# Routing token ids instead of token rows to the experts of a fused attention and mixture-of-experts kernel

## The chip, the cores and the metric

The kernel runs on one core of a Trainium2 chip. A core has a matrix engine (PE, with its weight loads shown apart as PEld), a vector engine (DVE), a scalar engine (ACT), a general engine (POOL), and a sync engine (SP), which here only issues DMAs. Each engine runs its own instructions in the order in which the program gives them. DMAs that SP issues are made into transfers by hardware; indirect DMAs, whose row numbers stand in a tile, are issued by POOL, which itself works out the transfers. All of them are carried by the same 16 DMA engines.

The metric is the device time of one execution in microseconds (us), lower is better. All times below are in us.

## The reference

The first half is a gated linear attention over a state of 48 x 48 for each of 4 batches and 8 heads, 768 steps long. Its output, taken as 3072 tokens of 384 numbers, goes into a mixture of 8 experts with one expert for each token. A token whose skip score is not positive passes unchanged.

```
for t in range(S):                                     # S = 768; B, H, D = 4, 8, 48
    state = alpha[:, :, t, :, None] * state + einsum('bhd,bhe->bhde', k[:, :, t], v[:, :, t])
    y[:, :, t] = einsum('bhd,bhde->bhe', q[:, :, t], state)
x = y.transpose(0, 2, 1, 3).reshape(B * S, H * D)      # 3072 tokens of 384

do_compute = x @ w_skip > 0
xc = x[do_compute]
e_idx = argmax(xc @ w_gate);  gate_w = softmax(xc @ w_gate)[e_idx]
for e in range(8):                                     # w1[e]: 384 x 1024, w2[e]: 1024 x 384
    h = maximum(xc[e_idx == e] @ w1[e], 0)
    y[e_idx == e] = gate_w * (h @ w2[e])
out = x;  out[do_compute] = xc + y
```

## The kernel before

**Attention.** The 3072 tokens are 24 blocks of 128 (`NT`), and one pass of the loop in `static_path` (lines 780 to 848) handles one block. `load(i + 4)` fetches the inputs of a later block on SP: for the first five blocks one transfer of 112 rows of 1541 numbers (L217), afterwards two (L220), and the 128 x 384 values (L223). There are five input buffers. `decay(i + 3)` scans the decay factors twice on DVE (L233, L241) and multiplies keys and queries by them, on POOL from block 2 on (L244, L245). `scores`, `causal`, `inter`, `intra`, `outer` and `carry` are the attention itself, on PE, DVE and ACT. `rows(i - 1)` turns a block's result into 128 rows of 384 numbers, copies them to the tile `x` (ACT, L343) and writes them to `out` (SP, L345). So every token's row is in `out` before any expert runs, as the result of a token that no expert handles, and in the tile `x` as well.

**Routing.** `route_expert` or `route_one` finds the expert and the gate of each token; `route_rank` and `route_slot` number the tokens of an expert one after the other. Expert e owns a stretch of the scratch tensor `xs` in DRAM; its first 256 places (`CAP`) are its slots. `scatter(i)` (POOL, L474) sends the 128 rows of `x`, 386 numbers each (384 of the token, its row number, its gate), to their slots by an indirect DMA. A slot that gets no token must hold a row number that is out of range, so that nothing is written for it at the end: `clear_pieces` fills all slots beforehand with `empty`, whose row number is `OFF`. It makes `empty` on POOL (L146, L147) and issues eight transfers on SP, two in each of the first four passes of the loop.

**Expert 0.** Most tokens of expert 0 are fetched early: in the last pass `early_rows` reads its 256 slots into `xr0` (SP, L435) as soon as the scatters of the first 21 blocks have landed. `early_turn` transposes them on PE (L449). The tokens of the last three blocks (`LATE` on) are added to the transposed tile by a product with a 0/1 matrix (`late_rows`, `hot`), and needn't come through DRAM. For this the tile `slots0` holds the slot number of each column.

**Experts.** `gather(e)` reads the 256 slots of an expert into `xr`, two transfers of 128 rows on SP (L530). Expert 1 and 0 come first, and then `gather(e + 2)` at the head of each expert's pass. An expert's pass is, in the written order of each engine:

- `gather(e + 2)`;
- four times `up(e, g)`: 18 matrix products of about 0.12 us on PE into one of three `ps_h` buffers, then `hh` on ACT (L581) and `hl` on DVE (L582), which frees the buffer; behind each, two pieces of `split_pieces(e + 1)`: ACT makes the high part of a raw weight piece (L508) and DVE or POOL the low part (L512). Of the 12 pieces POOL does numbers 1, 3, 6, 8 and 11; 0 to 5 belong to `w1`, 6 to 11 to `w2`;
- `turn(e + 1)`: transposes the next expert's rows (PE, L557);
- four raw `w1` pieces of expert e + 2 on SP (L492, 128 x 768 numbers each). They go into the buffer that the raw `w1` of expert e + 1 occupies, and are issued when all its readers on ACT, DVE and POOL are done;
- twice `down(e, j)`: 24 products on PE (L593), then `o` = gate times the result plus the token's row on DVE (L596), and an indirect DMA of 128 rows to `out` by the row numbers (POOL, L598); two more weight pieces behind each, and one step of `guard`;
- four raw `w2` pieces of expert e + 2 on SP.

`guard` looks for decay factors out of the range that the fast path may use. It reads all of `alpha` in eight portions through a single buffer (SP, L541, 128 x 1152 numbers each), and ACT passes over each portion twice (L545); the next portion is issued when both are done. It spans experts 0 to 4.

The order is the written one (`manual_schedule`). Waits follow from what instructions read and write. Scatters to one tensor are declared independent of each other (`disjoint`), and readers of `xs` are made to wait for them by `after`.

## Time and profile before

| | |
|---|---|
| time, three runs | 328.18, 332.03 (median), 335.56 |
| time of the profiled execution | 333.48 |
| its span in the profile | 331.8 |
| PE busy | 292.5 (88%) |
| DVE busy | 226.9 (68%) |
| POOL busy | 184.3 (56%) |
| ACT busy | 152.6 (46%) |
| moved by DMA | 66.15 MB, of these 4.83 MB by POOL's indirect DMAs |
| attention and routing | 0 to about 182 |
| the eight experts | about 182 to 325 |

A row of a timeline gives the start of an instruction from the start of the span, its duration, engine, line and operation, what it writes and reads, its shape, and how many such instructions were merged into the row. In square brackets stands the time for which the engine had been idle and what ended that. "SPq" is SP issuing a DMA: its duration is that of the issue, not of the transfer. A row of the windows gives for each engine the busy time in a stretch with the number of instructions, then the granted share of the PE clock, the mean share in which the 16 DMA engines were busy, and the rate in GB/s. The chain of waits follows the work that ended last back from the end.

### The profile page before, as it was taken

What the parts mean: (1) busy time and instruction counts of PE and PEld (TensorE: products, weight loads), DVE (VectorE), ACT (ScalarE), POOL (GpSimd) and SP (SyncE); (2) the same over time, 40 slices, a digit from 0 to 9 for tenths busy, and PEclk for the clock granted to TensorE, in tenths of its full rate; (3) what the DMA queues carried; (4) which work ended last, traced back from release to release, by engine and by line L of the source; (5) the groups of instructions that cost most, each with busy time, mean ns of one, the idle gap of its engine ahead of it and who ended that gap; (6) DMA issues with size and microseconds to landing.
All of it is one profiled execution on the core that took longest, in us unless ns stands there. A gap on an engine that the chain in (4) does not pass through costs nothing. (4 is left out here: it accounts for less than half of the span.)

```text
span 331.8 us, 7365 instructions
## 1 busy us (share of the span) xinstructions
PE 292.5 (88%) x2778; PEld 270.2 (81%) x2778; DVE 226.9 (68%) x453; ACT 152.6 (46%) x298; POOL 184.3 (56%) x205
## 2 busy tenths in 40 slices
PE   5877879998699986858898999999999999999991
PEld 5766768887588775646677999999999899999991
DVE  8995578899979999999437664738183555455320
ACT  5122422353435414402424657958595976455200
POOL 6093432589888988866524445444655355464311
PEclk9578785999879999995959999999999999999997
DMA  7949999999976867773546574949688586751000
GB/s 230 281 133 250 252 283 250 223 257 224 236 148 152 183 157 176 197 193 97 155 125 201 166 235 157 398 137 379 215 285 314 193 331 229 242 172 63 12 19 29
DMA packets 29420, 66.15 MB, mean 199 GB/s; under 512 B 4466, under 2 KB 15456, under 8 KB 29376
## 3 DMA queue, kind: packets, MB, share of 16 engines
q1 hardware_dynamic: 26816, 60.76, 63.6%
q0 software_dynamic: 2560, 4.83, 4.2%
q8 instruction: 24, 0.39, 0.5%
q14 instruction: 20, 0.16, 0.2%
HBM read 52.87 MB, written 15.77 MB: 207 GB/s over the span
## 5 line engine op out<-in xcount | busy, mean ns | idle before, releaser
L254 PE MATMUL ps_s<-qka 48*128 48x128 f32 x384 | 31.8, 308 | 23.8 <-POOL qka L244 12.0
L244 POOL TENSOR_TENSOR qka<-qka,sfx 112x512 f32<-112x512 f32 x22 | 27.7, 1257 | 42.4 <-DVE sfx L241 30.7
L254 PEld LDWEIGHTS ps_s<-qka 48*128 48x128 f32 x384 | 26.9, 209 | 29.0 <-POOL qka L244 13.5
L582 DVE SCALAR_TENSOR_TENSOR hl<-ps_h,hh 128x512 fp32r<-128x512 f32 x32 | 22.1, 690 | 33.5 <-ACT hh L581 33.3
L593 PE MATMUL ps_o<-w2h,hh 128*128 128x384 f32 x128 | 43.6, 341 | 0.0
L598 POOL DMA_INDIRECT out_dram<-o,xr x16 | 18.6, 1162 | 45.0 <-DVE o L596 45.0
L593 PE MATMUL ps_o<-w2h,hl 128*128 128x384 f32 x128 | 43.0, 336 | 0.0
L593 PE MATMUL ps_o<-w2l,hh 128*128 128x384 f32 x128 | 43.0, 336 | 0.0
L233 DVE TENSOR_TENSOR_SCAN pfx<-qka,seed 112x516 f32<-112x516 f32 x24 | 34.0, 1418 | 11.0 <-DMA qka<-in_qka_dram 11.0
L343 ACT COPY x<-ps_g 128x384 f32<-128x384 f32 x23 | 11.0, 480 | 65.5 <-DVE logit L338 23.7
L512 POOL TENSOR_TENSOR w2l<-raw,w2h 128x512 fp32r<-128x512 f32 x24 | 31.2, 1302 | 13.5 <-ACT w2h L508 13.1
L474 POOL DMA_INDIRECT xs<-x,slot x24 | 29.9, 1244 | 12.2 <-DVE on L386 4.9
L577 PE MATMUL ps_h<-xh,w1h 128*128 128x256 f32 x192 | 34.2, 284 | 1.2 <-DVE hl L582 1.2
L310 ACT COPY xt<-ps_y 48x512 f32<-48x512 f32 x48 | 27.8, 580 | 13.6 <-PE ps_y L305 12.8
L577 PE MATMUL ps_h<-xh,w1l 128*128 128x256 f32 x192 | 33.8, 282 | 0.0
L241 DVE TENSOR_TENSOR_SCAN sfx<-qka,seedb 112x515 f32<-112x515 f32 x24 | 32.3, 1347 | 1.5
L577 PE MATMUL ps_h<-xl,w1h 128*128 128x256 f32 x192 | 33.3, 282 | 0.0
L305 PE MATMUL ps_y<-st,vt 128*48 128x128 f32 x384 | 32.9, 313 | 0.0
L512 POOL TENSOR_TENSOR w1l<-raw,w1h 128x512 fp32r<-128x512 f32 x16 | 22.3, 1395 | 18.7 <-issue 10.4
L581 ACT ACTIVATE hh<-ps_h 128x512 fp32r<-128x512 f32 x32 | 19.1, 597 | 27.6 <-PE ps_h L577 27.6
L261 DVE COPY_PREDICATED st<-mask,ps_s 128x1024 f32<-128x1024 uint8 x24 | 30.9, 1286 | 0.0
L596 DVE SCALAR_TENSOR_TENSOR o<-ps_o,xr 128x384 f32<-128x384 f32 x16 | 9.9, 616 | 30.3 <-PE ps_o L593 30.3
(141 smaller groups left out, 667.5 us busy)
## 6 DMA issues: line engine op xcount, KB each, us to landing
raw<-in_w_dram SPq DMA_DIRECT2D x64, 384.0 KB
qka<-in_qka_dram SPq DMA_DIRECT2D x38, 288.9 KB
vt<-in_v_dram SPq DMA_DIRECT2D x24, 192.0 KB
out_dram<-x SPq DMA_DIRECT2D x24, 192.0 KB
alpha<-in_nat_dram SPq DMA_DIRECT2D x8, 576.0 KB
xr<-xs SPq DMA_DIRECT2D x18, 193.0 KB
xs<-empty SPq DMA_DIRECT2D x8, 386.0 KB
qka<-in_first_dram SPq DMA_DIRECT2D x3, 674.2 KB
```

The lines of the kernel that those rows point to most:

```text
L233: nc.vector.tensor_tensor_scan(pfx[:PD].rearrange("p a t -> p (a t)"), w["qka"][:PD, 0:n], self.seed1[:PD], 0.0, ALU.mult, ALU.max)
L241: nc.vector.tensor_tensor_scan(sfx[:PD, 0:n - 1][:, ::-1], w["qka"][:PD, 2:AW][:, ::-1], seed[:PD, 2:AW][:, ::-1], 0.0, ALU.mult, ALU.add)
L244: (eng or nc.gpsimd).tensor_tensor(w["kh"][:PD], w["kh"][:PD], after, ALU.mult)
L254: nc.tensor.matmul(ps[:, h, p * P:(p + 1) * P], lhsT=kh[r, p, :], rhs=qh[r, p, :], start=True, stop=True)
L261: self.nc.vector.copy_predicated(w["st"], self.mask, w["ps"])
L305: nc.tensor.matmul(ps[h][64 * h:64 * h + D, p, :], lhsT=v[:, o:o + D], rhs=w["st"][:, h, p * P:(p + 1) * P], start=(i < B and p == 0), sto ...
L310: nc.scalar.copy(out=xt[r], in_=ps[h][r])
L474: ins = nc.gpsimd.indirect_dma_start(out=self.xs[:, :], out_offset=bass.IndirectOffsetOnAxis(ap=self.slot[:, i, :], axis=0), in_=x, in_off ...
L512: eng.tensor_tensor(lo[:, s], raw[:, s], hi[:, s].bitcast(F32), ALU.subtract)
L577: nc.tensor.matmul(ps[:, u, :], lhsT=a[:, k, f * P:(f + 1) * P], rhs=b[:, k, :], start=(n == 0), stop=(n == len(order) - 1))
L582: nc.vector.scalar_tensor_tensor(out=hl, in0=ps, scalar=0.0, in1=hh.bitcast(F32), op0=ALU.max, op1=ALU.subtract)
L593: nc.tensor.matmul(ps, lhsT=a[:, f, js], rhs=b[:, f, :], start=(n == 0), stop=(n == 3 * FT - 1))
```

## The change

The slots hold two numbers, a row number and a gate, instead of 386. `scatter` sends only those two columns of `x`. A reader of an expert's slots first fetches them on SP (`meta`, 128 x 2 x 2 numbers, one transfer instead of two) and then the token rows themselves: `fetch_rows` issues two indirect DMAs on POOL that read 128 rows each from `out` by the row numbers in `meta`. Row numbers out of range are skipped, so the receiving tiles are cleared once: `xr0` on POOL at the start, the three tiles `xrb` on DVE before the experts.

The slots of an expert are laid out anew (partition p holds slots 2p and 2p + 1), and `slots0` follows that.

The eight transfers of `clear_pieces` become one, `clear`, of 8 x 256 x 2 numbers. It is issued as a whole before the loop over the blocks, and followed on SP by three transfers that write zeros to the rows of `out` that belong to the last three blocks, since the early fetch names all of `out` as its source before these rows are written. The loop's calls that advanced the clearing are gone.

A fetch reads `out`, and so waits for what was written there before it (`rows`, and later the experts' results), and what is written there after it waits for the fetch.

```diff
@@ first_constants
-        self.xs = dram.tile([E * N, XW], F32, name="xs")
+        self.xs = dram.tile([E * N, 2], F32, name="xs")
@@ first_slots
-        nc.gpsimd.iota(slots0_i, pattern=[[1, CAP]], base=-int(BIG), channel_multiplier=0)
+        nc.gpsimd.iota(slots0_i, pattern=[[1, NB], [NB, P]], base=-int(BIG), channel_multiplier=0)
@@
-    def clear_pieces(self):
-        nc = self.nc
-        empty = self.const.tile([P, XW], F32, name="empty")
+    def slots(self, e0, e1):
+        return self.xs.rearrange("(e n) w -> e n w", e=E)[e0:e1, :CAP, :].rearrange("e (p j) w -> p e (j w)", j=NB)
+
+    def clear(self):
+        nc = self.nc
+        empty = self.const.tile([P, NB, 2], F32, name="empty")
         nc.gpsimd.memset(empty, 0.0)
-        nc.gpsimd.iota(empty[:, DM:DM + 1].bitcast(I32), pattern=[[0, 1]], base=OFF, channel_multiplier=0)
-        for e in range(E):
-            yield nc.sync.dma_start(out=self.xs[e * N:e * N + CAP, :].rearrange("(j p) w -> p j w", p=P),
-                                    in_=empty.unsqueeze(1).to_broadcast([P, NB, XW]))
+        nc.gpsimd.iota(empty[:, :, 0:1].bitcast(I32), pattern=[[0, NB]], base=OFF, channel_multiplier=0)
+        nc.sync.dma_start(out=self.slots(0, E),
+                          in_=empty.rearrange("p j w -> p (j w)").unsqueeze(1).to_broadcast([P, E, 2 * NB]))
+        for i in range(LATE, NT):
+            row = self.row(i)
+            nc.sync.dma_start(out=self.out[row:row + P, :], in_=self.xr0[:, 0, :])
@@ attention_pools
+        self.xr0 = self.late.tile([P, NB, DM], F32, name="xr0")
+        nc.gpsimd.memset(self.xr0, 0.0)
@@ early_rows
-        for j in range(NB):
-            ins = nc.sync.dma_start(out=self.xr0[:, j, :], in_=self.xs[j * P:(j + 1) * P, :])
-            self.after(ins.ins, "xs")
-            self.early.append(ins.ins.name)
+        meta = self.late.tile([P, NB, 2], F32, name="meta0")
+        ins = nc.sync.dma_start(out=meta.rearrange("p j w -> p (j w)"), in_=self.slots(0, 1).rearrange("p e w -> p (e w)"))
+        self.after(ins.ins, "xs")
+        self.early = [ins.ins.name]
+        self.fetch_rows(self.xr0, meta)
+
+    def fetch_rows(self, xr, meta):
+        for j in range(NB):
+            self.nc.gpsimd.indirect_dma_start(
+                out=xr[:, j, :], out_offset=None, in_=self.out[:, :],
+                in_offset=bass.IndirectOffsetOnAxis(ap=meta[:, j, 0:1].bitcast(U32), axis=0),
+                bounds_check=N - 1, oob_is_err=False)
@@ scatter
-            in_=x, in_offset=None, bounds_check=E * N - 1, oob_is_err=False)
+            in_=x[:, DM:DM + 2], in_offset=None, bounds_check=E * N - 1, oob_is_err=False)
@@ expert_pools
+        self.xrb = [self.mp.tile([P, NB, DM], F32, name=f"xr{i}", bufs=1) for i in range(3)]
+        for t in self.xrb:
+            self.nc.vector.memset(t, 0.0)
@@ gather
-        xr = self.mp.tile([P, NB, XW], F32, name="xr", bufs=3)
-        for j in range(NB):
-            s = e * N + j * P
-            ins = self.nc.sync.dma_start(out=xr[:, j, :], in_=self.xs[s:s + P, :])
-            self.after(ins.ins, "xs")
-        self.ew[e] = dict(xr=xr)
+        xr = self.xrb[e % len(self.xrb)]
+        meta = self.mp.tile([P, NB, 2], F32, name="meta", bufs=4)
+        ins = self.nc.sync.dma_start(out=meta.rearrange("p j w -> p (j w)"),
+                                     in_=self.slots(e, e + 1).rearrange("p e w -> p (e w)"))
+        self.after(ins.ins, "xs")
+        self.fetch_rows(xr, meta)
+        self.ew[e] = dict(xr=xr, meta=meta)
@@ down
-        nc.vector.scalar_tensor_tensor(out=o, in0=ps, scalar=xr[:, j, DM + 1:DM + 2], in1=xr[:, j, 0:DM],
+        nc.vector.scalar_tensor_tensor(out=o, in0=ps, scalar=meta[:, j, 1:2], in1=xr[:, j, :],
...
-            out_offset=bass.IndirectOffsetOnAxis(ap=xr[:, j, DM:DM + 1].bitcast(U32), axis=0),
+            out_offset=bass.IndirectOffsetOnAxis(ap=meta[:, j, 0:1].bitcast(U32), axis=0),
@@ static_path
-            clear = self.clear_pieces()
+            self.clear()
             for i in range(NT):
                 if i + 4 < NT:
                     self.load(i + 4)
-                advance(clear, 2)
```

More of the change, by code (lines that the diff above doesn't have):

```diff
@@ L340, in rows @@
         x = self.xp.tile([P, XW], F32, name="x")
-        row = i % B * S + i // B * P
+        row = self.row(i)
         nc.gpsimd.iota(x[:, DM:DM + 1].bitcast(I32), pattern=[[0, 1]], base=row, channel_multiplier=1)
@@ L586, in down @@
         w2h, w2l = (a.rearrange("p (f m) -> p f m", m=DM) for a in self.wt[e]["w2"][:2])
-        xr = w["xr"]
+        xr, meta = w["xr"], w["meta"]
         js = slice(j * P, (j + 1) * P)
@@ L757, in static_path @@
         ends = {g[1] - 1: g for g in groups}
-        pending, split, fetch, clear = [], iter(()), iter(()), iter(())
+        pending, split, fetch = [], iter(()), iter(())
         def advance(it, n):
```

5 lines of the change are left out of this document (3 added, 2 removed).

## The prediction

> **What bounds the kernel now.** I read the profile's first page, then the windows by stage, the timelines of SP, POOL, ACT and DVE around the edits, and the chain of waits.
>
> ```profile
> span 331.8 us, 7365 instructions
> ```
>
> ```profile
> core 0: us, PE busy (x) PEld busy (x) DVE busy (x) ACT busy (x) POOL busy (x), PEclk, DMA share, GB/s
> 0.00:20.00 20.00, 13.23 (x100) 11.80 (x100) 18.47 (x29) 6.79 (x13) 9.36 (x20) 0.74 0.80 222
> 60.00:160.00 100.00, 84.44 (x1134) 71.93 (x1133) 93.48 (x197) 37.89 (x78) 81.68 (x100) 0.93 0.77 186
> 182.00:235.00 53.00, 53.00 (x380) 52.81 (x379) 30.58 (x47) 38.73 (x72) 26.78 (x21) 1.00 0.72 252
> 235.00:261.00 26.00, 24.84 (x184) 24.43 (x182) 11.96 (x19) 18.40 (x33) 11.65 (x9) 1.00 0.63 221
> 261.00:325.00 64.00, 63.89 (x446) 63.41 (x446) 32.42 (x55) 31.41 (x60) 28.08 (x22) 1.00 0.46 164
> ```
>
> Attention is DVE's (93.48 of 100 us). The experts are PE's: from 182 on it idles only 26 - 24.84 = 1.16 us. So whatever makes PE wait there is paid in full, unless it ends before that 1.16. The profiled execution took 333.48, 1.45 over the median 332.03; I sum against 333.48 and subtract 1.45.
>
> **Part 1, the start.** Two edits pull apart. Eight clearing transfers (128 x 2 x 386 x 4 bytes = 395 KB each, 3.16 MB) become one small one and three of zeros (197 KB each). And the new clearing is issued as a whole ahead of the loop, so ahead of the load of block 4.
>
> ```profile
> 8.69 0.33 SPq L217 DMA_DIRECT2D qka<-in_first_dram  x1
> 20.44 2.37 SPq L149 DMA_DIRECT2D xs<-empty  x2
> ```
>
> ```profile
> 19.79 0.41 POOL L146 MEMSET empty<- 128x386 f32 x1
> 20.28 0.13 POOL L147 IOTA empty<- 128x1 int32 x1
> ```
>
> ```profile
> 20.23 1.22 DVE L233 TENSOR_TENSOR_SCAN pfx<-qka,seed 112x516 f32<-112x516 f32 x1
> 29.05 1.23 DVE L233 TENSOR_TENSOR_SCAN pfx<-qka,seed 112x516 f32<-112x516 f32 x1 [3.25 <-DMA qka<-in_qka_dram]
> ```
>
> ```profile
> DVE pfx L233 <- DMA qka<-in_qka_dram: 10.7, 4, 3.2
> ```
>
> The load of block 4 is issued at 8.69, and SP then stands until POOL has made `empty` (20.41). POOL's queue keeps that place; with a smaller fill I put it at 20.1. Now the load of block 4 (112 x 1541 x 4 = 690 KB) stands behind that wait and behind 590 KB of zeros. The first window moved 222 GB/s at a share of 0.80, 278 when busy: 1.28 MB take 4.6. With 2.4 of fixed delay (the shortest landing quoted in part 2) block 4 is there at 20.1 + 4.6 + 2.4 = 27.1, where DVE took it up at 20.23: 6.9 late. Against that, the four waits for loads of blocks 5 to 8, 10.7 together, were beside the clearing. The first (3.25) falls into the lag anyway. If all four go, the start gains 10.7 - 6.9 = 3.8; if only the first goes, it loses 3.6. From block 6 on, a load is issued behind the row output of an earlier block, which the lag delays too, so I don't take the whole: 2 gained. The smaller scatters (24 x 198 KB gone) I cost at nothing: DVE's 93% from 60 to 160 hides them. `xr0`'s fill on POOL lies under the first loads.
>
> **Part 2, expert 0's early rows.** One transfer on SP and two indirect DMAs on POOL replace two on SP.
>
> ```profile
> 173.08 0.80 SPq L435 DMA_DIRECT2D xr<-xs  x2
> ```
>
> ```profile
> L474 POOL DMA_INDIRECT xs<-x,slot x24: 971/1048/2007, 62.3 to 183.1; - x24
> DMA to landing us min/median/max: 2.4/4.6/5.9
> ```
>
> ```profile
> 177.71 0.61 PE L449 MATMUL ps_s<-ident,xr 128*128 128x128 f32 x4
> 179.95 0.69 PE L449 MATMUL ps_s<-ident,xr 128*128 128x128 f32 x4
> ```
>
> No gather is in this trace; the nearest is the scatter of 128 rows. The row numbers land at 173.08 + 2.4 = 175.5, POOL issues at 175.5 and 176.7, and the rows land 2.4 to 4.6 later: 177.9 to 180.1 and 179.1 to 181.3. PE reads them at 177.71 and 179.95. So 0 to 1.35; I take 0.4. Queued behind the fetch are POOL's low parts of blocks 22 and 23 (about 0.5 late, under PE's own wait) and SP's row outputs and last two raw pieces, needed an expert later.
>
> **Part 3, the expert loop.** Here a wait is added that was not there: POOL must have the row numbers before it can issue. Behind the two fetches in POOL's order stand its pieces of the next expert's weights.
>
> ```profile
> 185.80 2.70 SPq L530 DMA_DIRECT2D xr<-xs  x6
> 191.68 2.13 SPq L492 DMA_DIRECT2D raw<-in_w_dram  x4
> 204.28 1.84 SPq L492 DMA_DIRECT2D raw<-in_w_dram  x4
> 206.23 0.99 SPq L530 DMA_DIRECT2D xr<-xs  x2
> 209.67 1.76 SPq L492 DMA_DIRECT2D raw<-in_w_dram  x4
> 214.95 7.53 SPq L541 DMA_DIRECT2D alpha<-in_nat_dram  x2
> 222.58 1.86 SPq L492 DMA_DIRECT2D raw<-in_w_dram  x4
> ```
>
> ```profile
> 196.96 1.19 POOL L598 DMA_INDIRECT out_dram<-o,xr  x1 [3.24 <-DVE o L596]
> 198.18 1.30 POOL L512 TENSOR_TENSOR w2l<-raw,w2h 128x512 fp32r<-128x512 f32 x1
> 205.36 1.38 POOL L512 TENSOR_TENSOR w1l<-raw,w1h 128x512 fp32r<-128x512 f32 x1 [1.71 <-ACT w1h L508]
> 206.89 1.56 POOL L512 TENSOR_TENSOR w1l<-raw,w1h 128x512 fp32r<-128x512 f32 x1 [0.15 <-ACT w1h L508]
> ```
>
> ```profile
> 201.04 1.26 ACT L545 ACTIVATE over<-alpha,lim 128x1152 bf16<-128x1152 f32 x1 [5.33 <-DMA alpha<-in_nat_dram]
> 219.34 1.26 ACT L545 ACTIVATE over<-alpha,lim 128x1152 bf16<-128x1152 f32 x1 [3.39 <-DMA alpha<-in_nat_dram]
> 221.98 0.58 ACT L581 ACTIVATE hh<-ps_h 128x512 fp32r<-128x512 f32 x1
> 228.07 0.62 ACT L508 CAST w2h<-raw 128x512 fp32r<-128x512 f32 x1 [0.93 <-DMA raw<-in_w_dram]
> 228.91 0.62 ACT L508 CAST w2h<-raw 128x512 fp32r<-128x512 f32 x1 [0.22 <-DMA raw<-in_w_dram]
> ```
>
> ```profile
> 207.95 1.64 DVE L512 TENSOR_TENSOR w1l<-raw,w1h 128x512 fp32r<-128x512 f32 x2
> 222.59 0.69 DVE L582 SCALAR_TENSOR_TENSOR hl<-ps_h,hh 128x512 fp32r<-128x512 f32 x1 [3.52 <-ACT hh L581]
> ```
>
> ```profile
> 200.19 8.66 PE ps_h L577 x72
> 281.31 0.66 PE ps_x L557 x6
> 298.94 0.66 PE ps_x L557 x6
> ```
>
> These rows show a ring of waits with little to spare. SP issues raw `w1` at 209.67, just after DVE's last reading of the old one (207.95 + 1.64 = 209.59; POOL's had ended at 208.45). Behind it stands `alpha` (214.95), which lands 4.39 later; ACT reads it twice, and only then turns to `hh` (221.98), for which PE's buffers wait. Then come the next `alpha` and raw `w2` (222.58). From raw `w2` to raw `w2` that is 222.58 - 204.28 = 18.3; PE needs 298.94 - 281.31 = 17.63 for an expert. Now the same ring after the change, counted from the first raw `w2` issue:
>
> - the row numbers are issued at 206.23 - 204.28 = 1.95, behind four raw pieces in the same queue. Those pieces land 0.84 apart (ACT finds them at 228.07 and 228.91), the first 5.5 after its issue, so the fourth at 8.0 and the row numbers with it. Bounds: 4.35 if a small transfer passes the queue, 8.0 if not. I take 8.0, since the pieces themselves come in order;
> - POOL's two fetches, 198.18 - 196.96 = 1.22 each: 10.45;
> - POOL's two `w1` pieces, 1.38 + 1.56: 13.4. They now end last, and release raw `w1` there (before: 5.4);
> - `alpha` is issued 1.85 after, at 15.25. It lands 4.39 + 1.5 later, as the four pieces ahead carry 4 x 0.84 = 3.36 and had 1.85 of start: 21.15;
> - from the first reading to the next raw `w2` 222.58 - 219.34 = 3.24: 24.4.
>
> So the ring takes 24.4, 6.8 more than PE needs. It turns three times (`alpha` ends in expert 4). Its first delay: the row numbers of expert 1 are issued at 185.80 and land at 188.2; six fetches (experts 1, 0, 2) take 7.3, two pieces 2.94, so raw `w1` goes out at 198.5 instead of 191.68, `alpha` lands at 198.5 + 1.85 + 5.9 = 206.3 instead of 201.04, 5.2 late. `hl` of expert 1 ends 3.94 after the first reading (222.59 + 0.69 - 219.34), at 210.2; PE wants that buffer for its fourth group at 200.19 + 3 x 8.66 / 4 = 206.7: 3.5 of stall. Then 6.8 in each of the experts 2, 3 and 4, together 23.9; less the 1.16 of before, 22.7. The first turn of expert 1 may come up to 2.5 late, and DVE's three fills put `hl` of expert 0 up to 2.3 back; both go into the 3.5. Experts 5 to 7 have no `alpha`, and their raw pieces have a whole expert's time: nothing.
>
> By the Trainium skill (TensorE: Matmul & The Clock Gate, Part 1) an idle window of about 3.4 us halves the PE clock until about 3.4 us of work have passed. The 1.16 of idle time kept 1.00 here, which neither confirms nor denies it; stalls of 6.8 would be long enough. The next stall would absorb the loss, except after the last: an estimate of 1.7 more.
>
> **Sum.** 333.48 - 2 + 0.4 + 22.7 = 354.6; less 1.45, 353.
>
> **Rivals.**
>
> *Row numbers pass the queue.* They land at 4.35, raw `w1` goes out at 9.75, `alpha` lands at 17.5, and the ring takes 20.7: stalls of 3.5 + 3 x 3.1 - 1.16 = 11.6, 342 in all. For it: 2 KB against 393 KB. Against: the order in which raw pieces land.
>
> *Fetches are dear.* If each costs POOL 2.0, the longest scatter, the first delay grows by 6 x 0.78 = 4.7 and the ring by 1.6: 8.2 + 3 x 8.4 - 1.16 = 32.2; with 0.6 more in part 2, 363. For it: the 2007 ns; against: the median of 1048. The Trainium skill (SBUF — State Buffer, "SBUF: two separate sides") says that some DVE operations lock POOL out while it writes the transfers of a DMA.
>
> *Not slower: POOL has room.* If its `w1` pieces still end by 209.59, the ring stays at 18.3 and only the start counts: 330, and 321 if all 10.7 are won and block 4 is not late. This decides where the fetches end by 209.59 - 2.94 = 206.65. For it: POOL is busy 26.78 of 53 us. Against: the row numbers aren't issued before 206.23, so the pieces would have to stand ahead of the fetches, and the written order has them behind.
>
> **How the numbers follow.** Forecast 0.58 (346 to 360), row numbers pass 0.18, dear fetches 0.14, POOL has room 0.10. About 2% (325.4 to 338.6) is what a measurement can tell from no change. Faster than that is only the better end of the last rival, 0.04; within it the rest of that rival and the low tail of the first, 0.09; slower 0.87. The range runs from 339, the first rival with a good start, to 366, where the dear fetches meet a start that gains nothing.
>
> **What would show it.** SP issues block 4's load after 20, and DVE waits some 6 us for it; the waits for blocks 5 to 8 shrink. POOL idles before the fetch of experts 3 to 6 until the row numbers land; raw `w1` follows POOL's second piece, not DVE's; ACT waits longer for `alpha`, and PE idles before the fourth group of experts 1 to 4. I am wrong if POOL doesn't wait there, or if PE stays busy from 182 on.

## The result: 13.6% slower, and the profile after

The changed kernel takes 377.72 us (median of 4 runs) where the kernel before takes 332.57 beside it: ratio 1.1356, interval 1.1051 to 1.1662. The direction was forecast, the size was not: 353, with a range up to 366. Two of its four executions, the profiled one (380.15) among them, ran some 1% longer than the other two, and a ratio leaves such executions out. So times are compared by the ratios, and the rows below for where things stand.

The page of the changed kernel: its span, PE's busy tenths and granted clock, and what the transfers moved, in 40 slices.

```profile
span 378.4 us, 7392 instructions
...
PE   6860989987889978499797969759589399997991
...
PEclk9585796999977999956989989969989889999997
...
GB/s 240 138 52 189 191 250 193 164 233 204 211 145 114 174 142 180 128 115 63 93 125 77 205 172 162 264 206 85 233 231 182 149 206 216 168 194 212 29 4 36
```

The windows by stage, with stretches that answer to those of before (experts from 193 on):

```profile
core 0: us, PE busy (x) PEld busy (x) DVE busy (x) ACT busy (x) POOL busy (x), PEclk, DMA share, GB/s
0.00:20.00 20.00, 14.45 (x100) 12.93 (x100) 18.48 (x28) 6.15 (x12) 9.38 (x20) 0.74 0.63 179
60.00:160.00 100.00, 83.45 (x1127) 71.39 (x1126) 91.26 (x181) 37.29 (x74) 75.07 (x93) 0.93 0.78 171
193.00:246.00 53.00, 44.24 (x308) 43.39 (x307) 29.32 (x37) 24.12 (x45) 26.71 (x23) 0.96 0.51 168
246.00:315.00 69.00, 53.17 (x328) 52.75 (x329) 40.79 (x43) 42.91 (x78) 27.49 (x23) 0.88 0.53 179
315.00:371.00 56.00, 53.26 (x373) 51.99 (x371) 33.75 (x44) 21.55 (x40) 27.01 (x22) 1.00 0.41 140
```

PE now idles in the experts, 8.8 us of the first 53 and 15.8 of the next 69, and its clock falls to 0.88. The experts' first product begins at 193.2 (182.3 before) and their last ends at 370.7 (324.9): 10.9 us lost ahead of them, 34.9 in them.

**The start.** SP's timeline, then DVE's for the first scan of block 4:

```profile
20.78 0.41 SPq L152 DMA_DIRECT2D xs<-empty  x1
21.23 1.54 SPq L157 DMA_DIRECT2D out_dram<-xr  x3
22.82 0.44 SPq L230 DMA_DIRECT2D qka<-in_first_dram  x1
```

```profile
33.34 1.23 DVE L246 TENSOR_TENSOR_SCAN pfx<-qka,seed 112x516 f32<-112x516 f32 x1 [12.37 <-DMA qka<-in_first_dram]
```

The load of block 4, issued at 8.69 before, goes out at 22.82, and its data are taken up 10.5 us later. In that time the transfers nearly stand: the page's third slice (18.9 to 28.4 us) shows 52 GB/s.

**The way into the experts.** POOL's timeline has the two fetches of expert 0's early rows and the last scatter, SP's the row numbers of the experts, and the view of the slots' transfers how long these took to land:

```profile
185.12 1.06 POOL L454 DMA_INDIRECT xr<-out_dram,meta  x1 [2.48 <-DMA meta<-xs]
186.49 1.02 POOL L454 DMA_INDIRECT xr<-out_dram,meta  x1 [0.31 <-issue]
...
192.50 0.97 POOL L494 DMA_INDIRECT xs<-x,slot  x1 [0.31 <-issue]
```

```profile
197.88 1.28 SPq L552 DMA_DIRECT2D meta<-xs  x3
```

```profile
DMA to landing us min/median/max: 1.7/5.5/10.6
```

That view takes in all transfers of the slots, three reads of row numbers among them. The scatters alone whose landing is recorded (20 of the 24) took 5.4 us in the median, 3.4 to 10.6; of those of 1544-byte rows (9 of the 24) it was 4.6, 2.4 to 5.9. So a scatter of 8-byte rows landed no sooner. The last one, issued at 192.50, landed 5.1 us later (2.4 before), and SP can ask for the row numbers only at 197.88.

**The ring.** One turn of it in expert 2, in the timelines of SP, POOL, ACT and PE (PE's first three rows are of passes 0 and 1; pass e is the work on expert e):

```profile
223.69 1.83 SPq L512 DMA_DIRECT2D raw<-in_w_dram  x4
225.57 0.43 SPq L552 DMA_DIRECT2D meta<-xs  x1
236.91 1.75 SPq L512 DMA_DIRECT2D raw<-in_w_dram  x4
238.76 10.49 SPq L565 DMA_DIRECT2D alpha<-in_nat_dram  x2
249.35 0.88 SPq L512 DMA_DIRECT2D raw<-in_w_dram  x2
```

```profile
231.94 1.05 POOL L454 DMA_INDIRECT xr<-out_dram,meta  x1 [14.12 <-DMA meta<-xs]
233.30 1.01 POOL L454 DMA_INDIRECT xr<-out_dram,meta  x1 [0.31 <-PE ps_o L617]
234.33 2.55 POOL L532 TENSOR_TENSOR w1l<-raw,w1h 128x512 fp32r<-128x512 f32 x2
```

```profile
246.12 1.25 ACT L569 ACTIVATE over<-alpha,lim 128x1152 bf16<-128x1152 f32 x1 [10.82 <-DMA alpha<-in_nat_dram]
```

```profile
203.81 0.55 PE L581 MATMUL ps_x<-ident,xr 128*128 128x128 f32 x3 [1.77 <-DMA xr<-out_dram,meta]
205.33 0.55 PE L581 MATMUL ps_x<-ident,xr 128*128 128x128 f32 x3 [0.98 <-DMA xr<-out_dram,meta]
224.44 1.01 PE L601 MATMUL ps_h<-xh,w1h 128*128 128x256 f32 x3 [3.70 <-DVE hl L606]
250.10 1.01 PE L601 MATMUL ps_h<-xh,w1h 128*128 128x256 f32 x3 [6.41 <-DVE hl L606]
```

POOL stands 14 us before the fetch; its two `w1` pieces follow and release raw `w1` (236.91); `alpha` comes behind that, and PE waits 6.4 for the evictions that ACT does after it. The waits of the whole execution, totals first:

```profile
POOL xr L454 <- DMA meta<-xs: 67.2, 6, 14.5
ACT over L569 <- DMA alpha<-in_nat_dram: 43.7, 4, 12.0
...
PE ps_h L601 <- DVE hl L606: 21.8, 4, 6.4
```

### The profile page after: what moved, and what is told of

The parts are those of the page before. It is cut to its first block, busy times and chain, and to the rows that moved or that the text cites. A ratio compares the mean times of both kernels' runs of the same rounds, so it can differ in the third digit from the quotient of the medians.

```text
span 378.4 us, 7392 instructions
## 1 busy us (share of the span) xinstructions
PE 304.8 (81%) x2778; PEld 281.3 (74%) x2778; DVE 256.1 (68%) x456; ACT 152.9 (40%) x298; POOL 200.0 (53%) x224
## 4 chain that ended last, share of the span: by engine, by line
PE 30%; DMA 21%; POOL 16%; DVE 15%; issue 9%; ACT 4%; SPq 3%; POOLq 0%; DVEq 0%; ACTq 0%
PE ps_h L601 8%; DMA alpha<-in_nat_dram 8%; PE ps_o L617 7%; POOL w1l L532 4%; DVE sfx L254 4%; PE ps_s L267 3%; PE ps_g L350 3%; DMA qka<-in_qka_dram 3%; DVE pfx L246 3%; DMA qka<-in_first_dram 3%; PE ps_y L296 3%; DMA raw<-in_w_dram 3%; DVE st L274 3%; SPq L512 2%; POOL xr L454 2%
## 5 line engine op out<-in xcount | busy, mean ns | idle before, releaser
L454 POOL DMA_INDIRECT xr<-out_dram,meta x18 | 18.8, 1047 | 77.8 <-DMA meta<-xs 67.2
L267 PE MATMUL ps_s<-qka 48*128 48x128 f32 x384 | 33.6, 323 | 30.2 <-POOL qka L257 22.6
L267 PEld LDWEIGHTS ps_s<-qka 48*128 48x128 f32 x384 | 28.7, 223 | 36.2 <-POOL qka L257 24.6
L601 PE MATMUL ps_h<-xh,w1h 128*128 128x256 f32 x192 | 37.2, 303 | 21.8 <-DVE hl L606 21.8
L606 DVE SCALAR_TENSOR_TENSOR hl<-ps_h,hh 128x512 fp32r<-128x512 f32 x32 | 22.0, 686 | 42.4 <-ACT hh L605 42.4
L601 PEld LDWEIGHTS ps_h<-xh,w1h 128*128 128x128 f32 x192 | 30.6, 206 | 22.9 <-DVE hl L606 22.7
L532 DVE TENSOR_TENSOR w2l<-raw,w2h 128x512 fp32r<-128x512 f32 x24 | 43.5, 1812 | 2.3 <-ACT w2h L528 2.3
L246 DVE TENSOR_TENSOR_SCAN pfx<-qka,seed 112x516 f32<-112x516 f32 x24 | 32.1, 1338 | 15.2 <-DMA qka<-in_first_dram 12.4
L494 POOL DMA_INDIRECT xs<-x,slot x24 | 31.3, 1306 | 13.1 <-DVE slot L436 6.8
L569 ACT ACTIVATE over<-alpha,lim 128x1152 bf16<-128x1152 f32 x16 | 20.2, 1259 | 43.9 <-DMA alpha<-in_nat_dram 43.7
L601 PE MATMUL ps_h<-xh,w1l 128*128 128x256 f32 x192 | 36.0, 297 | 0.0
L601 PE MATMUL ps_h<-xl,w1h 128*128 128x256 f32 x192 | 35.1, 295 | 0.0
```

The source lines that it names most:

```text
L246: nc.vector.tensor_tensor_scan(pfx[:PD].rearrange("p a t -> p (a t)"), w["qka"][:PD, 0:n], self.seed1[:PD], 0.0, ALU.mult, ALU.max)
L267: nc.tensor.matmul(ps[:, h, p * P:(p + 1) * P], lhsT=kh[r, p, :], rhs=qh[r, p, :], start=True, stop=True)
L454: self.nc.gpsimd.indirect_dma_start(out=xr[:, j, :], out_offset=None, in_=self.out[:, :], in_offset=bass.IndirectOffsetOnAxis(ap=meta[:, j ...
L494: ins = nc.gpsimd.indirect_dma_start(out=self.xs[:, :], out_offset=bass.IndirectOffsetOnAxis(ap=self.slot[:, i, :], axis=0), in_=x[:, DM:D ...
L532: eng.tensor_tensor(lo[:, s], raw[:, s], hi[:, s].bitcast(F32), ALU.subtract)
L601: nc.tensor.matmul(ps[:, u, :], lhsT=a[:, k, f * P:(f + 1) * P], rhs=b[:, k, :], start=(n == 0), stop=(n == len(order) - 1))
```

## The experiments

Each is an edit of the changed kernel. "Experts" is the time from the first product of expert 0 to the last product of expert 7, in the profiled execution; block 9 is where DVE begins the first scan of that block; the ratio is to the kernel before, run beside it on the same chip. "All together" is the row numbers in one transfer, fetches not ordered against scatters, and the mended start. TensorE, VectorE and ScalarE in the expectations are PE, DVE and ACT.

| kernel | ratio (interval) | block 9 | experts begin | experts take |
|---|---|---|---|---|
| before | 1 | 56.5 | 182.3 | 142.6 |
| changed | 1.1356 (1.1051–1.1662) | 62.5 | 193.2 | 177.5 |
| fetches later in the pass | 1.0800 (1.0747–1.0852) | 63.1 | 190.6 | 162.3 |
| row numbers in one transfer | 1.0540 (1.0488–1.0593) | 62.7 | 191.4 | 153.5 |
| and fetches not ordered against scatters | 1.0636 (1.0529–1.0743) | 62.4 | 190.9 | 151.4 |
| no `alpha` | 1.0718 (1.0601–1.0834) | 62.7 | 190.4 | 156.3 |
| load of block 4 first | 1.1153 (1.1060–1.1247) | 56.8 | 188.7 | 177.6 |
| clear in rows of 2 KB | 1.1150 (1.1061–1.1239) | 58.0 | 186.7 | 179.5 |
| start mended | 1.1029 (1.0904–1.1155) | 50.9 | 179.9 | 178.8 |
| all together | 1.0313 (1.0202–1.0424) | 50.2 | 179.9 | 153.7 |
| and the first pass reordered | 1.0201 (1.0143–1.0258) | 49.9 | 178.4 | 150.3 |
| and `alpha` one expert later | 1.0000 (0.9937–1.0062) | 50.0 | 180.1 | 145.2 |

### The ring: fetches later, row numbers at once, no `alpha`

The theory is the prediction's: POOL stands for the row numbers with its pieces of the weights behind, and so raw weights and `alpha` go round late. The rival: it is the fetches' own time. First the fetches move behind POOL's two `w1` pieces.

```diff
 gather
-        self.fetch_rows(xr, meta)
 static_path, before the passes
             for e in (1, 0):
                 self.gather(e)
+                self.fetch_rows(self.ew[e]["xr"], self.ew[e]["meta"])
 static_path, behind the four groups of the first product
+                if e + 2 < E:
+                    self.fetch_rows(self.ew[e + 2]["xr"], self.ew[e + 2]["meta"])
                 if e + 1 < E:
                     self.turn(e + 1)
```

> The changed kernel, but in each expert's pass POOL's two fetches for expert e + 2 stand behind its pieces of w1 (ahead of the turn) instead of at the head of the pass; the transfer of the row numbers stays where it is. If the ring of waits does the damage (POOL held by the row numbers, raw w1 released late, alpha late), raw w1 is again released by about 5.4 us after raw w2, the ring falls from 25.6 to about 18.5, PE no longer idles before the fourth group of experts 2 to 4, and the time falls by about 20 to 28, to 350 to 358. If it is the fetches' own time on POOL or their load on the DMA engines, POOL has as much to do as before, and the time stays above 368.

Measured 362.65, between the two. In the experts the wait for row numbers is down to 12.2 us, but a new one stands in its place; POOL's waits in the experts show it:

```profile
POOL out_dram L621 <- DMA xr<-out_dram,meta: 18.1, 4, 6.0
```

The scatter of the expert's output now comes right behind a fetch of other rows of `out`, and is ordered behind its landing. The order on POOL matters, then, and the fetch has a second tie, to `out`.

Next the row numbers of all experts come by one transfer, and the fetches stay at the head of the pass.

```diff
 gather
-        meta = self.mp.tile([P, NB, 2], F32, name="meta", bufs=4)
-        ins = self.nc.sync.dma_start(out=..., in_=self.slots(e, e + 1)...)
+        if not self.ew:
+            self.metas = self.mp.tile([P, E, NB, 2], F32, name="meta", bufs=1)
+            ins = self.nc.sync.dma_start(out=..., in_=self.slots(0, E))
+            self.after(ins.ins, "xs")
+        meta = self.metas[:, e]
```

> The changed kernel, but the row numbers of all eight experts are read by one transfer ahead of the first fetch; the fetches keep their place at the head of each pass. It takes the wait for the row numbers away and leaves the fetches in front of the w1 pieces. If the wait is what counts, POOL's idle time before the fetches of experts 3 to 7 (67 us in all) is gone, the ring falls to 18.5 to 20 and the time to 347 to 358. If the fetches' place and their 2.4 us are enough, the ring stays above 22 and the time above 365.

353.95: the experts take 24 us less with the fetches where they were, so it was not the fetches but the wait for their row numbers. What is left of POOL's waiting is the tie to `out`, here before the fetch for expert 3:

```profile
220.63 1.05 POOL L454 DMA_INDIRECT xr<-out_dram,meta  x1 [2.86 <-DMA out_dram<-o,meta]
```

Experts' rows are distinct, so this tie can go, for the fetches of the expert part:

```diff
 fetch_rows
-            self.nc.gpsimd.indirect_dma_start(
+            ins = self.nc.gpsimd.indirect_dma_start(
...
+            if hasattr(self, "ew"):
+                self.disjoint(ins.ins, "out")
```

> The row numbers of all experts come by one transfer ahead of the first fetch, as in the run before with that edit (353.95 us against 335.7 for the kernel before), and in addition a fetch of rows of `out` is no longer ordered against the experts' scatters into `out` (they touch different rows). Wait theory: what was left in passes 1 to 6 of that run (22.1, 18.7, 18.1, 18.9, 19.1 and 17.6 us against 17.7) is the fetch that stands on POOL until the scatter before it has landed (2.86 us at the fetch for expert 3), with the shares of the split behind it. Without it passes 1 to 6 take 17.7 to 18.3 us each and the kernel 345 to 349 us. Traffic theory: the rest is the fetches' own time on POOL and on the transfers, which both kernels have; then passes 1 to 6 stay as they were and the time is 352 to 355 us.

A miss: 352.17, within the traffic theory's range, and no gain over the run before this one (ratios 1.0636 and 1.0540, with intervals that overlap). From the third on the passes are near what the wait theory asks (17.6, 19.2, 18.4, 18.0, 17.7), but their sum, 90.9, is close to the 91.4 of the run before, whose pass 5 took 18.1 and not the 19.1 of the expectation. So this wait lay beside other work. The rest lies in the first two passes, 20.6 and 22.7, and POOL's timeline shows what stands in the way:

```profile
198.11 1.05 POOL L454 DMA_INDIRECT xr<-out_dram,meta  x1 [7.02 <-PE ps_h L604]
...
204.82 1.00 POOL L454 DMA_INDIRECT xr<-out_dram,meta  x1 [0.30 <-issue]
205.85 2.55 POOL L534 TENSOR_TENSOR w1l<-raw,w1h 128x512 fp32r<-128x512 f32 x2
```

Six fetches in a row, from 198.1 to 205.8, stand ahead of POOL's first share of expert 1's weights. (The row names PE as the releaser; the row numbers landed just ahead.)

Last, the reading of `alpha` is left out of the changed kernel.

```diff
-                    check = self.guard()
+                    check = iter(())
```

> The changed kernel without the reading of alpha that tests its range (left out: the test whether alpha lies within its bounds). The row numbers of each expert are still loaded by their own transfer behind the raw weights. Ring theory: a turn of the ring is the landing of the row numbers plus the landing of alpha plus what stands between them on the queue and on POOL; measured 25.7 us per expert where TensorE needs 17.7. Without alpha's 7.3 us the ring is 18.4 us, so that the stalls of 6.4 us in experts 2 to 4 and most of the 3.7 us in expert 1 are gone: passes 2 to 5 take 17.7 to 19 us in place of 26, and the kernel 346 to 357 us (375 less 19 for the stalls, up to 6 for the late end and some us of clock). Row-number theory: the fetch behind its own row numbers holds POOL for 14 us whatever else stands on the queue, and alpha only fills that time: the fetches wait as before, passes 2 to 5 stay over 23 us, and the kernel takes over 365 us.

355.71, in the ring theory's range, but the ring is not 18.4, and passes 4 and 5 are over its 19 us. SP's and POOL's rows for a turn:

```profile
229.54 8.58 SPq L512 DMA_DIRECT2D raw<-in_w_dram  x8
238.29 0.40 SPq L552 DMA_DIRECT2D meta<-xs  x1
250.66 9.73 SPq L512 DMA_DIRECT2D raw<-in_w_dram  x8
```

```profile
245.47 1.29 POOL L454 DMA_INDIRECT xr<-out_dram,meta  x1 [9.12 <-DMA meta<-xs]
```

A turn takes 250.66 - 229.54 = 21.1: without `alpha` the row numbers stand behind eight raw pieces in place of four, which gives back 2.7 of the 7.3. So `alpha` adds 4.6 to a turn, and the row numbers' landing (7.2) stays. At 3.4 over PE's need the ring overtakes PE only later: passes 1 to 3 take 17.7 at most, passes 4 to 6 21.0, 19.7 and 22.6.

### The start: load first, clear in rows, zeros later, all three

The theory is that the load of block 4 is late because it stands behind the clearing in SP's queue; the rival, that the small pieces slow whatever comes behind them. First the load goes ahead of the clear.

```diff
+            self.load(4)
             self.clear()
             for i in range(NT):
-                if i + 4 < NT:
+                if 4 < i + 4 < NT:
```

> The changed kernel, but the load of block 4 is issued ahead of the clearing. If its place behind the clearing costs the start its time, DVE's wait of 12.4 for block 4 goes, the waits for blocks 5 to 8 stay small since the large clearing is gone, block 9 is taken up at about 46 to 49 instead of 62.5, and the time falls by 10 to 15. If the clearing itself clogs the DMA engines (its 1024 pieces of 16 bytes, or the zeros), the wait moves to block 5, and the time falls by 5 at most.

The rival held, as far as the wait goes: block 4 starts at 20.9 (20.2 before the change), and DVE's wait is now at block 5:

```profile
34.07 1.23 DVE L246 TENSOR_TENSOR_SCAN pfx<-qka,seed 112x516 f32<-112x516 f32 x1 [7.50 <-DMA qka<-in_qka_dram]
```

Next the clear is written as 8 rows of 2 KB in place of 1024 pieces of 16 bytes, at its place.

```diff
-        empty = self.const.tile([P, NB, 2], F32, name="empty")
+        empty = self.const.tile([E, CAP, 2], F32, name="empty")
... (the fill and the transfer follow that shape)
```

> The changed kernel, but the clearing writes the slots of each expert as one row of 2 KB (8 pieces) instead of 1024 pieces of 16 bytes; its place and the zeros are unchanged. If the small pieces clog the DMA engines, the load of block 4 lands about 6 instead of 10.5 after its issue, DVE's wait for it falls from 12.4 to 7 to 8, and the time by about 4. If the zeros or the place alone count, the landing stays at 10 to 11.

```profile
28.87 1.23 DVE L246 TENSOR_TENSOR_SCAN pfx<-qka,seed 112x516 f32<-112x516 f32 x1 [7.89 <-DMA qka<-in_first_dram]
```

Issued at 23.70, the load of block 4 is taken up 5.2 us later, with the zeros still ahead of it; 10.5 in the changed kernel. (By their times neither of these two runs can be told from the changed kernel: both ratios lie inside its interval.) The counterpart leaves the 16-byte pieces and moves the zeros to block 12.

> The changed kernel with the three blocks of zeros for the last rows of `out` written at block 12 in place of behind the clear; the clear in 1024 pieces of 16 bytes stays ahead of the load of block 4. If the zeros are the larger part of the 10.5 us that this load took to land, block 4 starts by 25 to 27 us (33.3 in the changed kernel). If the 16-byte pieces are, it starts at 30 to 32 us: the load is issued 1.6 us sooner and lands as late as before behind the pieces.

```profile
32.17 1.23 DVE L248 TENSOR_TENSOR_SCAN pfx<-qka,seed 112x516 f32<-112x516 f32 x1 [11.21 <-DMA qka<-in_first_dram]
```

The load is issued at 21.23 and taken up 10.9 later; the clear itself, issued at 20.79, lands 8.45 later in this trace. So the 1024 pieces of 16 bytes are what holds the load, for some 5.5 us, and the zeros cost their issue time. Whether the number of the pieces counts or their size, no run here separates. (One execution; its time of 382.67 is not compared.) Now both, with the clear behind the load of block 7:

```diff
-            self.clear()
             for i in range(NT):
                 if i + 4 < NT:
                     self.load(i + 4)
                 if i == 3:
+                    self.clear()
                     fetch = self.weight_pieces(0)
+                if i == 12:
+                    self.zeros()
```

> The start alone is changed: the slots are cleared by one transfer of eight rows of 2 KB in place of 1024 pieces of 16 bytes, issued behind the load of block 7 in place of ahead of that of block 4, and the three blocks of zeros for the last rows of `out` are written at block 12. Small-piece theory: the loads of blocks 4 to 8 then meet nothing in the transfer engines; block 4 starts at 20 to 21 us (33.3 in the changed kernel, 20.2 before), block 9 at 53 to 57 (62.5 and 56.5), the experts at 183 to 186 (193.2 and 182.3), and the kernel takes 364 to 370 us. Rival: the first blocks' loads are the limit (the loss moves on to later blocks, as it did when the load alone was put ahead): block 9 stays over 59 and the kernel over 371.

The small-piece theory holds, and the trace is better than expected: block 9 at 50.9, the experts at 179.9, 13.3 us ahead of the changed kernel and 2.4 ahead of the kernel before. SP issues block 4's load early, and DVE waits for loads 3.0 us between 18 and 64 us where the kernel before waits 10.7:

```profile
9.42 0.33 SPq L232 DMA_DIRECT2D qka<-in_first_dram  x1
```

```profile
DVE pfx L248 <- DMA qka<-in_qka_dram: 3.0, 3, 1.5
```

The time, 366.9, is in the range that was expected, 3.3% or some 11 us below the changed kernel by the ratios, whose intervals overlap. It gains less than the start does, since the experts take 1.3 us more here.

By the Trainium skill (DMA: Bandwidth & Descriptors, Specifications) pieces below 512 bytes don't reach the full rate and are read, changed and written back. Reading and writing back is not shown by any run here; what the rows show, and the page does not state, is that such pieces hold up the load behind them.

### All together, and the first pass

The run with all edits also sets the row buffers to zero in the attention part in place of 2.3 us of DVE at the start of the experts.

```diff
 expert_pools
-        self.xrb = [self.mp.tile([P, NB, DM], F32, name=f"xr{i}", bufs=1) for i in range(3)]
-        for t in self.xrb:
-            self.nc.vector.memset(t, 0.0)
 static_path
+        self.xrb = [self.x0.tile([P, NB, DM], F32, name=f"xr{i}") for i in range(3)]
+        self.nc.gpsimd.memset(self.xrb[0], 0.0)
...
                 if i == 8:
                     self.first_slots()
+                    for t in self.xrb[1:]:
+                        self.nc.gpsimd.memset(t, 0.0)
 attention_pools
-        self.xr0 = self.late.tile([P, NB, DM], F32, name="xr0")
+        self.xr0 = self.xrb[0]
```

> The edits together: one transfer for the row numbers of all experts, fetches not ordered against the scatters, the start as in the run of the start alone, and the buffers for the rows set to zero in the attention part in place of at the start of the experts. If the three places (start, transition, ring) are all of the loss and independent, the gains add: 375 less 27 (ring and scatter wait), less 7 to 10 (start), less about 2 (the clears of 2.3 us ahead of the first expert's work): 336 to 340 us, against about 333 to 336 for the kernel before. If the first pass of the experts (21 to 25 us in every variant so far, 17.7 before) has its own cause in the fetches that follow the last scatter of slots, 340 to 345 us.

342.43, as the second case has it: start and ring add, the first two passes (23.8 and 22.0) stay. Next, POOL's order in pass 0 is changed.

```diff
 gather
-        self.fetch_rows(xr, meta)
+        if e > 2:
+            self.fetch_rows(xr, meta)
 static_path
                     self.up(e, g)
                     advance(split, 2)
+                    for k in {(0, 0): (1, 0), (0, 3): (2,)}.get((e, g), ()):
+                        self.fetch_rows(self.ew[k]["xr"], self.ew[k]["meta"])
-                if e + 1 < E:
+                if 0 < e < E - 1:
                     self.turn(e + 1)
...
                     self.down(e, j)
+                    if e + j == 0:
+                        self.turn(1)
```

> The run with all edits together, and in the first pass of the experts the order of the fetches changed: after the first group of the first product POOL issues the fetch for expert 1, then that for expert 0, and the fetch for expert 2 only behind the four groups and its shares of the split; the turn of expert 1 comes between the two second products of expert 0 in place of ahead of both. Order theory: what is left of the loss against the kernel before is that six fetches in a row (8 us of POOL) stand ahead of POOL's shares of the split for expert 1, and that the turn of expert 1 waits for the last scatter, the row numbers and the fetch in sequence: passes 0 and 1 take 23.8 and 22.0 us where 17.7 is the measure. They then take 18 to 20 us each, and the kernel 334 to 338 us where all edits together took 342.4 (before 333.0). Chain theory: the sequence scatter, row numbers, fetch is simply too long for the first pass whatever the order on POOL; passes 0 and 1 stay at 42 us or more in sum, and the time over 340 us.

339.57: pass 0 falls from 23.8 to 19.0, pass 1 stays at 23.4. Their sum, 42.4, is what the chain theory asked, but not for its reason, since pass 0 is near its measure; and the time is just under its 340. So neither theory had that. ACT's and PE's timelines show what is in the way:

```profile
204.06 1.25 ACT L571 ACTIVATE over<-alpha,lim 128x1152 bf16<-128x1152 f32 x1 [8.05 <-DMA alpha<-in_nat_dram]
```

```profile
208.04 0.99 PE L603 MATMUL ps_h<-xh,w1h 128*128 128x256 f32 x3 [4.00 <-DVE hl L608]
```

It is the first link of the old ring: `alpha`, behind raw weights that POOL released late. So the test of alpha starts one expert later (and the flag is worked out in pass 6).

```diff
-                if e == 0:
+                if e == 1:
                     check = self.guard()
...
-                    if (e, g) in ((5, 0), (5, 2)):
+                    if (e, g) in ((6, 0), (6, 2)):
                         self.must_redo(g)
...
-                    advance(check, 1)
+                    advance(check, 1 if e else 0)
```

> The run with the order of the first pass changed, and in addition the test of alpha's range begins with expert 1 in place of expert 0 and ends with expert 5 (the flag is worked out in pass 6 in place of pass 5). In the run before it pass 1 still took 23.4 us: the first wait of ScalarE for alpha (8.05 us at 204.06) stands ahead of the evictions of expert 1's first product and ahead of the release of the next raw weights. Alpha theory: with the test moved pass 1 takes 18 to 19 us and the kernel 333 to 336 us, no longer than the kernel before (332.8). Late-weights theory: the raw weights of expert 2 are 3 us later than before in any case, because the fetches stand ahead of POOL's share of the split that releases them; pass 1 stays over 21 us and the kernel over 337 us.

The alpha theory holds: pass 1 takes 17.6. The medians of all executions are 335.11 and 333.47, and the ratio is 1.0000 (0.9937 to 1.0062). The windows of the experts are again near those of the kernel before:

```profile
180.10:235.00 54.90, 54.34 (x389) 54.10 (x388) 31.95 (x49) 33.81 (x63) 35.71 (x30) 1.00 0.64 215
235.00:261.00 26.00, 24.54 (x183) 24.13 (x181) 11.82 (x19) 19.44 (x35) 16.55 (x14) 1.00 0.67 227
261.00:325.30 64.30, 63.45 (x440) 62.76 (x438) 31.79 (x53) 35.56 (x66) 29.78 (x24) 1.00 0.49 173
```

PE idles 2.9 us there in place of 1.3. The experts take 2.6 us more than before the change and begin 2.2 earlier. So nearly all of the loss was in waits, not in the fetches' work, and with it gone nothing is gained over the kernel before: the experts are bound by PE with either way of bringing the rows. The kernel before was not run with the test of `alpha` moved, so what that edit is worth without the change stays open.

### Wider slots

To test whether the scatters land late because their rows are small, the run with all edits got slots of 512 bytes.

```diff
-            in_=x[:, DM:DM + 2], in_offset=None, ...
+            in_=x[:, XW - P:XW], in_offset=None, ...
... (`xs`, its clear and its reads follow that width)
```

> The run with all edits together, with slots of 512 bytes (the last 128 values of the token's row, id and gate at their end) in place of 8 bytes; only id and gate are read back. It asks for the landing of the slot scatters alone. Small-row theory: a row of 8 bytes lands later than a long one because it is small: with 512 bytes the landing goes from 5.1 us (median, longest 8.3) back to the 4.6 (5.9) of the 1544-byte rows of the kernel before, or below. Traffic theory: the landing is set by what else the transfers carry (raw weights, loads of the blocks), so that it stays at 5 to 6 us median. The row numbers are read in 8-byte pieces here, which lengthens the way into the experts by 1 to 4 us; the time is 342 to 348 us in either case.

Inconclusive: the trace of this run has no landings. The time is the same (342.47 and 342.43). SP asks for the row numbers 3.4 us after the last scatter's issue (181.3, 184.7) in place of 6.3 (179.5, 185.8), which leans to the small rows; one trace does not settle it.

## Why the prediction was wrong in size

The forecast was 353 and the time 377.7, 24.7 more. By the start of the experts the forecast had -1.6 (-2 and +0.4), the trace +10.9: 12.5 of it. In the experts it had 22.7, the trace 34.9: 12.2 of it.

**Part 1, "2 gained": 8.4 lost, wrong in sign.** The step that failed is "block 4 is there at 27.1". It was there at 33.3, 6.2 later. Of these, 2.7 are the issue of the load, at 22.82 for 20.1: POOL's fill was 0.7 later than assumed, and SP takes 2.0 to issue the clear and the zeros ahead of it. The other 3.5 are the transfer. It was costed by its 1.28 MB at the mean rate, 7.0 us for all, and the 16 KB clear was taken as nothing; behind that clear it took 10.5, and 5.2 behind the same clear in 8 rows. The second half held: the four waits for blocks 5 to 8 fell from 10.7 to 1.3. Of the 13.1 us by which block 4 was late, block 9 still shows 6.0 (62.5 and 56.5). By the end of attention it is 8.4 (PE's last counting products, at 185.21 and at 176.79 before); why it grows by 2.4 on the way is open. The mended start shows the gain that the forecast had in mind, 2.4 at the start of the experts.

**Part 2, "0.4": 2.4.** The row numbers are asked for at 182.45, and PE's timeline has the readings of the two halves:

```profile
188.14 0.71 PE L469 MATMUL ps_s<-ident,xr 128*128 128x128 f32 x4 [1.79 <-DMA xr<-out_dram,meta]
...
189.51 0.86 PE L469 MATMUL ps_s<-ident,xr 128*128 128x128 f32 x4 [0.37 <-DMA xr<-out_dram,meta]
```

The rows are there 5.7 and 7.1 after the request; 4.8 to 7.0 and 6.0 to 8.2 were forecast. What failed is PE's side. It is ready 3.9 us after the request, not the 4.63 of before, and waits 1.79 and 0.37, where the kernel before waits 1.35 between the halves for DVE (`hot`). That puts the second half 1.1 further behind. The other 1.3 is PE's clock, which the forecast did not have in this place. The window behind the two waits has it at 0.50:

```profile
189.90:193.30 3.40, 3.40 (x18) 3.40 (x18) 0.73 (x5) 0.37 (x1) 2.79 (x3) 0.50 0.74 205
```

From the second half to the first product of expert 0 PE takes 3.65 us (from 189.51) in place of 2.36 (from 179.95).

**Part 3, the ring, step by step**, counted from the raw `w2` issue at 223.69:

| step | forecast | measured |
|---|---|---|
| row numbers issued | 1.95 | 1.88 |
| POOL's first fetch | 8.0 | 8.25 |
| fetches done | 10.45 | 10.64 |
| raw `w1` issued | 13.4 | 13.22 |
| `alpha` issued | 15.25 | 15.07 |
| `alpha` read | 21.15 | 22.43 |
| next raw `w2` | 24.4 | 25.66 |

The mechanism and the other steps were right; the term of the ring that was mis-sized is the landing of `alpha`, 7.36 for 5.9. The other errors are in what lies round the ring. By passes, against the kernel before:

- passes 1 to 4 together, 28.3 for 22.7 (3.5 and 3 x 6.8, less the 1.16). The three turns of the ring, from the end of one stall at 224.44 to that at 301.14, take 76.7 for 73.2: 3.5 of the error. Behind the last stall 2.3 are lost to the clock (see below);
- pass 0, 3.3 for nothing: "both go into the 3.5" failed. The turn of expert 1 waits 1.77 + 0.98 in pass 0, and the stall of 3.70 comes on top in pass 1, since it hangs on POOL's pieces and not on PE's own delay. Behind this stands a step that the forecast did not have, the landing of the smaller scatters, costed at nothing: the row numbers of expert 1 are asked for 5.4 after the last scatter's issue (192.50, 197.88), the rows themselves 2.7 after it before (183.11, 185.80);
- passes 5 to 7, 3.4 for "nothing", 3.1 of it in pass 6: the row numbers still bind POOL with no `alpha` in the way, as SP's rows for the last expert's weights show: row numbers asked for at 323.01, raw `w1` released 11.8 later. "A whole expert's time" was counted from PE, not along SP's queue.

```profile
321.09 1.75 SPq L512 DMA_DIRECT2D raw<-in_w_dram  x4
323.01 0.33 SPq L552 DMA_DIRECT2D meta<-xs  x1
334.79 8.82 SPq L512 DMA_DIRECT2D raw<-in_w_dram  x8
```

**The clock.** PE's granted clock fell from 1.00 to 0.88 between 246 and 315 us, where the stalls of 5.6 to 6.4 are, and was 1.00 again after. The Trainium skill (TensorE: Matmul & The Clock Gate, Part 1) has an idle window of about 3.4 us halve it; the rows agree for these stalls. But the clock was also halved behind the two waits of 1.79 and 0.37 in part 2, so here shorter waits were enough. As forecast, the loss costs nothing of its own inside the ring: the next stall takes it up. Behind the last stall nothing does. From the start of its fourth group pass 4 takes 13.5 us to its end where the kernel before takes 11.2 in its undisturbed passes: 2.3, for which the forecast named an estimate of 1.7 and left it out of its sum.

**The rivals.** "Row numbers pass the queue" is out: they land in 5.5 us, behind the raw pieces. "Fetches are dear" is out as a cause: a fetch takes POOL 1.36 us from one to the next (231.94, 233.30; 1.22 forecast), and row numbers in one transfer brought 24 us back with all the fetches kept. "POOL has room" is what the last run comes to once the row numbers are there, the first pass is in order and `alpha` comes later; the room was there, the order was not.

## What to carry to other kernels

An index that has to be fetched before data can be fetched puts two landings in sequence on the engine that issues the gather, and everything behind it in that engine's order pays: load indices for all stages at once, well ahead, and put the gather behind work that others wait for. Where transfers share a queue with bulk loads, cost a small one by what stands ahead of it and by its pieces, not by its bytes alone. And when one term of a prediction falls on a ring of waits, follow each link round it to the end, into the stages that seem to have time.

## What the runs showed of the hardware that was not expected

- 16 KB written in 1024 pieces of 16 bytes held up what came behind in the queue: a load of 690 KB was taken up 10.5 and 10.9 us after its issue behind them, 5.2 behind 8 rows of 2 KB.
- An indirect scatter of 128 rows of 8 bytes landed no sooner than one of 1544-byte rows: 5.4 us (3.4 to 10.6; 20 of 24 recorded) against 4.6 (2.4 to 5.9; 9 of 24), and POOL's issue takes 1.12 us for 1.05 (medians).
- An indirect gather of 128 rows of 1536 bytes costs POOL 1.05 us, with 0.3 to the next, and lands 3 us after its issue (median; 2.9 to 4.0).
- A fetch of 2 KB of row numbers landed 5.5 us after its issue behind four pieces of 393 KB, and 7.2 behind eight; one with no such piece just ahead of it (198.26) landed after 1.7.
- DVE's low part of a weight piece takes 0.69 us by itself. In the changed kernel 13 of its 56 took over 1.5 us, none before. The longest, from 233.6, 260.1, 284.9 and 311.2, took 4.5 to 5.0: they began beside POOL's fetch and three POOL pieces in a row, and ended about 0.5 after the last of these. The steps of the ring in the table do not run through them.
